# A fifth chunk of weights split early, buffers held per MLP, and a low part moved from POOL to DVE in a three-stage kernel

## The chip, the core and the metric

One core of one Trainium2 chip runs the whole program. The metric is the device time of one execution in microseconds. Engines are named as the profile names them: PE (matrix multiply), DVE (vector), ACT (activation), POOL (GpSimd) and SP (which here only issues DMAs).

## What is computed

Memory attention feeds an MLP with a sigmoid-gated unit, and that feeds a second, normalised and gated MLP. 4 batches of 576 tokens, 8 heads of 64 make 2304 tokens of width 512.

```python
a = softmax(phi, over the sequence)            # 32 memory slots
k_m, v_m = a^T k, a^T v
x = softmax(q k_m^T / 8) v_m                   # (2304, 512)
h = x @ w_in                                   # 512 -> 2048
x = (h * sigmoid(1.702 h)) @ w_out             # 2048 -> 512
xn = x / sqrt(mean(x*x) + 1e-6) * rms_g
g, val = xn @ w_gate, xn @ w_val               # 512 -> 1536
out = (silu(g) * val) @ w_out2                 # 1536 -> 512
```

The inputs are 64-bit floats; the kernel reads them as pairs of 32-bit words and makes 32-bit floats of them on the chip.

## The kernel before, in words

**Numbers.** A 32-bit float operand x is split into a high part (rounded to the format that PE multiplies) and a low part (x minus the high part), and each product is made of three matmuls: high by high, low by high, high by low. So every operand costs one rounding copy, nearly always on ACT, and one subtraction (`sub_lo`, line 125) on DVE or POOL.

**Weights.** `to_f32` makes one 512-column tile of 32-bit weights out of raw words: an absolute value on ACT (line 170), a clamp on POOL (171), and three bit operations on DVE (175, 179, 182). `w_conv` then splits it for the first MLP. For the second MLP a *chunk* is 128 columns of the gate and 128 of the value weights: `b_gate` and `b_val` call `to_f32`, `b_sums` adds four combinations (line 244, four DVE instructions; the second MLP multiplies its 2x2 blocks with seven products in place of eight), and `b_tile` four times splits one tile (`b_split`: a copy on ACT at line 223, a subtraction on POOL) and stores it to DRAM in `cache2`. `b_again` (line 271) loads such a chunk back with four DMAs. There are 12 chunks.

**First MLP.** It runs twice over 8 groups of 256 hidden columns: the first pass for batches 0 and 1, the second for batches 2 and 3. A unit is one group and one quarter of the pass's tokens (288): `a_g1` (line 564, gelu at 570, split at 572 and 125) and, one unit later, `a_g2` (line 593), whose four PSUM tiles DVE adds into `x2` (line 601). `vm_part` makes the attention-weighted first weights of the next group. The first pass has the splitting of the first MLP's weights beside it, the second loads them back.

**Side work.** In the second pass three steps of a generator, `second_side`, are put between `a_g1` and `a_g2` of each unit: the norm of batches 0 and 1 (`norm_sums`, `norm_side`), the seven operands of each batch (`x_side`: four subtractions at line 686, then five splits), and chunks 0 to 3.

**Second MLP.** `b_unit(c, b)` is chunk c for batch b: seven products of six matmuls (line 728), copies on ACT (757, 760, 762), additions on DVE (742, 765, 767), silu on ACT (768), two multiplications on DVE (746, 747), a split of the gated product (749 on ACT, and `sub_lo` into `pl`), and two stores to DRAM. The opening, `units_of(range(NG1), (0, 1), ...)`, runs chunks 0 to 3 for batches 0 and 1, while the list `more` prepares batches 2 and 3: `norm_sums(1)` (squares at 614, column sums on PE at 632), `norm_side` (line 668) and `x_side`. Then chunks 4 to 11 run for all four batches, each beside the splitting of the next chunk; then chunks 0 to 3 for batches 2 and 3; then the last product (line 795).

**Order.** The program is written as one sequence of steps, and the framework lays each engine's queue out ahead of time: of the instructions that are ready in its own simulation it takes the one written first, and `tc.high_priority(n)` counts an instruction as written n instructions earlier. On the chip each queue then runs in that fixed order. Units of the second pass are raised by 150, `vm_next` by 100, units of the opening by 400.

**Buffers.** Tiles come from pools with a fixed number of buffers. `cv` (4 tiles of 576 columns: conversions, norms, sums) and `w` (6 tiles of 1024 columns: split weights) last through the kernel; `vm` (4) belongs to the attention and the first MLP. Pools `raw`, `gf` and `gr` of the first MLP are released at its end, and those of the second (`rawb`, `tmp`, `gpp`, `nxp`, `xbp`) take the same memory, each tile waiting for the tiles that lay there.

Of the kernel before, what the change touches and what calls it, by code (L numbers as in the profile page):

```python
# [18 lines left out]
def kernel(  # L19
# [44 lines left out]
    NA = F1 // FG  # L64
    NB = F2 // FG
    NC2 = F2 // P
    NPRE = 4
    NG1 = 4
    TW = 2 * HALF
    TO = 384  # L70
# [5 lines left out]

    const = ctx.enter_context(tc.tile_pool(name="const", bufs=1))
    bigp = ctx.enter_context(tc.tile_pool(name="big", bufs=6))
    cvp = ctx.enter_context(tc.tile_pool(name="cv", bufs=4))
    dramp = ctx.enter_context(tc.tile_pool(name="dram", bufs=1, space=bass.MemoryType.DRAM))  # L80
    wp = ctx.enter_context(tc.tile_pool(name="w", bufs=6))
    w3p = ctx.enter_context(tc.tile_pool(name="w3", bufs=2))
    smp = ctx.enter_context(tc.tile_pool(name="sm", bufs=4))

# [2 lines left out]
    rawa = tc.alloc_tile_pool(name="rawa", bufs=3, side="right")  # L87
    gfp = tc.alloc_tile_pool(name="gf", bufs=3, side="right")
    grp = tc.alloc_tile_pool(name="gr", bufs=5, side="right")
    vmp = tc.alloc_tile_pool(name="vm", bufs=4, side="right")  # L90
    raws = [rawa]
    ps_mm = ctx.enter_context(tc.tile_pool(name="ps_mm", bufs=3, space=bass.MemoryType.PSUM))
    ps_acc = ctx.enter_context(tc.tile_pool(name="ps_acc", bufs=3, space=bass.MemoryType.PSUM))
    ps_att = ctx.enter_context(tc.tile_pool(name="ps_att", bufs=2, space=bass.MemoryType.PSUM))
# [9 lines left out]
        return bigp.tile([P, 4608], dt, tag="big", name=name)  # L104

    def wtile(name, dt=F32R):
        return wp.tile([P, 1024], dt, tag="w", name=name)

    def ttile(name, dt=F32):
        return cvp.tile([P, TW], dt, tag="cv", name=name)  # L110

    def psum(pool, name):
        tag = {id(ps_mm): "mm", id(ps_acc): "acc", id(ps_att): "att"}[id(pool)]
# [10 lines left out]
    def sub_lo(eng, lo, full, hi):  # L124
        eng.tensor_tensor(out=lo, in0=full, in1=hi.bitcast(F32), op=ALU.subtract)  # L125
# [1 line left out]


    cache = dramp.tile([NA * 4, P, 1024], F32, tag="cache", name="cache")
    cache2 = dramp.tile([NG1 * 4, P, 1024], F32, tag="cache2", name="cache2")  # L130
    pcache = [
        dramp.tile([2, NC2, P, PT], F32, tag=f"pcache{i}", name=f"pcache{i}") for i in range(2)
    ]
# [3 lines left out]
        return [(*key, w, i) for w in ("in", "out") for i in range(2)]  # L137

    def w_load(hf):
        raw = loaded[hf] = raws[0].tile([P, 1024], U32, tag="raw", name="raw_" + "_".join(map(str, hf)))  # L140
        if hf[0] == "b":
            c, w = hf[1:]
            src = {"gate": w_gate, "val": w_val, "o2": w_o2}[w]
            if w == "o2":
                nc.sync.dma_start(out=raw, in_=src[c * P : (c + 1) * P, :])
            else:
                nc.sync.dma_start(
                    out=raw.rearrange("p (k f) -> p k f", k=NE),
                    in_=src[:, 2 * c * P : 2 * (c + 1) * P].rearrange("(k p) f -> p k f", p=P),
                )  # L150
            return
        g, w, i = hf[2:]
        src = {"in": w_in, "out": w_out}[w]
        if w == "out":
            nc.sync.dma_start(out=raw, in_=src[g * FG + i * P : g * FG + (i + 1) * P, :])
        else:
            nc.sync.dma_start(
                out=raw.rearrange("p (k f) -> p k f", k=2),
                in_=src[2 * i * P : 2 * (i + 1) * P, 2 * g * FG : 2 * (g + 1) * FG].rearrange(
                    "(k p) f -> p k f", p=P  # L160
                ),
            )
# [55 lines left out]
    def b_split(c, j, x):  # L218
        n = 256 if j == 3 else 512
        y = b_wtile(c, j)  # L220
        if c >= NPRE:
            wt.setdefault(("b", c), {})[j] = y
        nc.scalar.copy(out=y[:, :n], in_=x)  # L223
        sub_lo(G, y[:, n:], x, y[:, :n])
        if c < NG1:
            nc.sync.dma_start(out=cache2[c * 4 + j][:, : 2 * n], in_=y.bitcast(F32))

    def b_gate(c):
# [21 lines left out]
    def b_steps(c):  # L250
        yield b_gate, c
        yield b_val, c
        yield b_sums, c
        for j in range(4):
            yield b_tile, c, j
# [42 lines left out]

    def ld_phi(u):
        b, g = u  # L300
        if b < 2:
            km = vmp.tile([P, 1024], F32, tag="vm", name=f"kmisc{b}_{g}")
        else:
            km = wtile(f"kmisc{b}_{g}", F32)
        kmisc[u] = km
        dst = km[:CP, 0:768].rearrange("p (t r x) -> p t r x", t=2, r=2)
        for t in range(2):
            nc.sync.dma_start(
                out=dst[:, blk(b, 2 * t) // 2],
                in_=phi[b, 4 * g + 2 * t : 4 * g + 2 * t + 2].rearrange(  # L310
                    "r (p c) m -> p r (c m)", c=C6
                ),
            )
# [204 lines left out]
    def vm_part(pr, g, c):  # L518
        wh, wl = wt["a", pr, g, "in"]
        vh, vl = vL[pr]  # L520
        if c == 0:
            vm[pr, g] = [
                vmp.tile([P, 1024], F32R, tag="vm", name=f"vm{pr}_{g}{x}").rearrange("p (b c f) -> p b c f", b=2, c=2) for x in "hl"
            ]
        hi, lo = vm[pr, g]
        lows = []
        ps = (ps_a("pvm") if start_up[0] else psum(ps_mm, "pvm")).rearrange("p (j f) -> p j f", j=2)
        for j in range(2):
            p_ = 2 * c + j
            w0 = slice(p_ * FG, (p_ + 1) * FG)  # L530
            for i, (a, w) in enumerate(((vh, wh), (vl, wh), (vh, wl))):
                nc.tensor.matmul(  # L532
                    ps[:, j], lhsT=a[:, p_], rhs=w[:, w0], start=(i == 0), stop=(i == 2)
                )


        for rows, bb, src in (
            (slice(0, 64), slice(0, 2), slice(0, 2)),
            (slice(64, 128), 1, 0),
            (slice(64, 128), 0, 1),  # L540
        ):
            o, x = (rows, bb, c), ps[rows, src]
            nc.scalar.copy(out=hi[o], in_=x)
            lows.append((lo[o], x, hi[o]))
        for o, x, h in lows:
            sub_lo(nc.vector, o, x, h)
        if c == 1:
            wt.pop(("a", pr, g, "in"))
# [168 lines left out]
    def b_unit(c, b):  # L717
# [26 lines left out]
        def late_2():  # L744
            prod(px, 6, 6, False, True)
            nc.vector.tensor_tensor(out=pf[:, 1], in0=pf[:, 1], in1=sg[:, 1], op=ALU.mult)
            nc.vector.tensor_tensor(out=pf[:, 0], in0=sg[:, 0], in1=px, op=ALU.mult)  # L747
            ph, pl = (gpp.tile([P, TW], F32R, tag="gp", name=x) for x in ("ph", "pl"))
            nc.scalar.copy(out=ph, in_=fv)  # L749
            sub_lo(G if b < 2 and c < NG1 else V, pl, fv, ph)  # L750
            n = slice((b % 2) * S, (b % 2) * S + S)
            for i, x in enumerate((ph, pl)):
                nc.sync.dma_start(out=pcache[b // 2][i, c, :, n], in_=x.bitcast(F32))
# [95 lines left out]
    def first(n):  # L849
        return tc.high_priority(n) if n else nullcontext()  # L850
# [34 lines left out]
    def second_side():  # L885
        for w in ("gate", "val"):
            yield w_load, ("b", 0, w)
        yield from norm_sums(0)
        yield from b_prep(0, 1)
        yield from norm_side(0)  # L890
        yield from x_side(0, 0)
        yield from b_prep(1, 2)
        yield from x_side(0, 1)
        yield from b_prep(2, 3)
        yield from norm_side(1)
        yield from b_steps(3)
        yield from x_side(1, 0)

    units = [(i, key, t) for i, key in enumerate(groups) for t in range(4)]
    order = [hf for key in groups[1:NA] for hf in halves(key)]  # L900
# [36 lines left out]
    def run(lo, hi, prev, side, per):  # L937
        nonlocal done
        for i, key, t in units[lo:hi]:
            if key == ("a", 1, 0) and t == 1:  # L940
                side, per = second_side(), 3
            if key == ("a", 1, 7) and t == 1:
                b_again(0)
            with first(150 if key[1] else 0):
                a_g1(*key[1:], t)
            if i + 1 < NA:
                w_conv(halves(groups[i + 1])[t])
                done += 1
                if done + ahead <= len(order):
                    w_load(order[done + ahead - 1])  # L950
            elif i + 1 < len(groups) and t in (0, 2):
                w_again((*groups[i + 1], "in" if t == 0 else "out"))
            if t == 2 and i + 1 < len(groups):
                vm_next(*groups[i + 1][1:], 0, 1)
            for s in islice(side, per):
                do(s)
            with first(150 if key[1] else 0):
                a_g2(*prev[1:])
            prev = (*key, t)
        a_g2(*prev[1:])  # L960
        return side

    side = run(8, len(units), ("a", 0, 1, 3), side, 2)
    for pool in (vmp, grp, gfp, rawa, kmp, vlp):
        pool.release()
    two = dict(side="right", reuse_waits="tile")
    raws[0] = rawb = tc.alloc_tile_pool(name="rawb", bufs=2, **two)
    tmp = tc.alloc_tile_pool(name="tmp", bufs=4, **two)
    gpp = tc.alloc_tile_pool(name="gp", bufs=3, **two)
    nxp = tc.alloc_tile_pool(name="nx", bufs=1, **two)  # L970
    xbp = tc.alloc_tile_pool(name="xb", bufs=2, **two)
    for s in (*side, *x_side(1, 1)):
        do(s)

    def units_of(cs, bs, steps, more):
# [55 lines left out]
    for g in range(2 * PT // TO):  # L1031
        p_out(g)
        for x in loads[2 * g + 3 : 2 * g + 5]:
            p_load(*x)
    for pool in (xbp, nxp, gpp, tmp, rawb):
        pool.release()


# [31 lines left out]
```

## Time and profile before

| what | value |
|---|---|
| time, median of 3 runs | 936.31 us (935.64 to 937.98) |
| time of the profiled execution | 942.23 us |
| its span (first to last instruction on the core) | 940.4 us |
| mean granted PE clock, share of full | 0.978 |
| busy share: PE, DVE, ACT, POOL | 91%, 63%, 48%, 52% |
| bytes moved by DMA | 170.14 MB |

The profile is of one execution. Busy is the time in which an engine runs instructions. A wait is an engine's idle time before an instruction, put down to what released it. In the rows below, "x12" counts instructions; "A:B" is a stretch in us from the start of the span; a clock of 1.00 is 2.4 GHz and 0.50 is 1.2 GHz, so a value between is a mix; the last two columns of a stretch are the busy share of the DMA engines and GB/s.

### The profile page before, as it was taken

How to read it: one execution, taken by the hardware profiler on the slowest of the kernel's cores; microseconds unless marked ns; L12 is line 12 of the kernel's file. 1: busy time of each engine (PE TensorE's matmuls, PEld its weight loads, DVE VectorE, ACT ScalarE, POOL GpSimd, SP SyncE). 2: the span in 40 equal slices, each digit the busy share in tenths (PEclk: the TensorE clock that was granted, in tenths of full speed). 3: DMA queues.
4: the chain of work that ended last, by engine and by line, in shares of the span. 5: the costliest groups of instructions: out<-in, count | busy, mean ns of one | idle time of the engine just before them, and what ended most of it. 6: DMA issues, size and time to landing. Idle time of an engine off the chain costs nothing.

```text
span 940.4 us, 16149 instructions
## 1 busy us (share of the span) xinstructions
PE 852.3 (91%) x6008; PEld 803.2 (85%) x6008; DVE 588.4 (63%) x1115; ACT 452.5 (48%) x995; POOL 487.0 (52%) x416
## 2 busy tenths in 40 slices
PE   3877998888999998989998769999999899999997
PEld 2766997887999998889998668999999898888886
DVE  5589777679865369895646989977776774000000
ACT  2257764564657665555455635555565453000000
POOL 2466798789966646863574886533351541000000
PEclk9998999899999999999999979999999999999999
DMA  9984358844532354453626135444446796966661
GB/s 221 229 260 157 114 178 225 261 148 157 171 118 108 109 195 146 168 181 124 223 101 200 64 108 187 150 172 162 148 147 239 255 359 226 344 221 220 211 196 33
DMA packets 86239, 170.14 MB, mean 181 GB/s; under 512 B 6544, under 2 KB 49552, under 8 KB 86160
## 3 DMA queue, kind: packets, MB, share of 16 engines
q1 hardware_dynamic: 81552, 152.33, 50.9%
q10 hardware_dynamic: 4608, 16.78, 4.6%
q8 instruction: 47, 0.77, 0.3%
q14 instruction: 32, 0.26, 0.1%
HBM read 111.94 MB, written 57.15 MB: 180 GB/s over the span
## 4 chain that ended last, share of the span: by engine, by line
PE 55%; DVE 15%; DMA 9%; POOL 7%; issue 5%; ACT 5%; SPq 2%; ACTq 0%; DVEq 0%; POOLq 0%
PE pg L795 16%; PE pg L593 12%; PE px L728 11%; PE pg L564 5%; PE pw L728 5%; POOL cv L171 3%; PE py L728 3%; DVE t L686 2%; DMA stage<-in_q_dram 2%; DVE cv L179 2%; DVE cv L182 2%; DMA raw_a_out<-in_moe_w_out_dram 2%; PE pvm L532 2%; POOL gr L125 2%; DVE x L668 2%
## 5 line engine op out<-in xcount | busy, mean ns | idle before, releaser
L593 PE MATMUL pg<-gr,a_outh 128*128 128x288 f32 x1024 | 239.0, 303 | 12.8 <-DVE x L601 9.7
L593 PEld LDWEIGHTS pg<-gr,a_outh 128*128 128x128 f32 x1024 | 177.3, 192 | 17.2 <-DVE x L601 12.9
L728 PE MATMUL px<-x,b_w 128*128 128x288 f32 x1152 | 175.3, 300 | 16.0 <-DVE pf L747 6.5
L728 PEld LDWEIGHTS px<-x,b_w 128*128 128x128 f32 x1152 | 161.0, 191 | 20.7 <-DVE pf L747 7.6
L125 POOL TENSOR_TENSOR gr<-gf,gr 128x288 fp32r<-128x288 f32 x128 | 117.5, 933 | 80.0 <-ACT gr L572 72.3
L171 POOL TENSOR_SCALAR cv<-cv 128x512 f32<-128x512 f32 x67 | 134.1, 2008 | 38.5 <-ACT cv L170 37.7
L593 PE MATMUL pg<-gr,a_outl 128*128 128x288 f32 x512 | 153.4, 300 | 0.0
L795 PE MATMUL pg<-o,p 128*128 128x512 f32 x648 | 147.6, 389 | 0.0
L795 PEld LDWEIGHTS pg<-o,p 128*128 128x128 f32 x648 | 121.5, 188 | 25.0
L601 DVE TENSOR_TENSOR x<-x,pg 128x288 f32<-128x288 f32 x224 | 97.0, 448 | 63.3 <-PE pg L593 62.1
L728 PE MATMUL pw<-x,b_w 128*128 128x288 f32 x576 | 92.9, 299 | 7.8 <-DVE sg L767 3.7
L593 PEld LDWEIGHTS pg<-gr,a_outl 128*128 128x128 f32 x512 | 98.8, 193 | 0.0
L728 PEld LDWEIGHTS pw<-x,b_w 128*128 128x128 f32 x576 | 82.0, 190 | 9.5 <-DVE sg L767 3.9
L572 ACT CAST gr<-gf 128x288 fp32r<-128x288 f32 x128 | 53.7, 433 | 40.7 <-PE pg L593 35.4
L570 ACT ACTIVATE gf<-pg 128x288 f32<-128x288 f32 x128 | 51.0, 409 | 44.1 <-POOL gr L125 26.6
L804 ACT COPY o<-pg 128x512 f32<-128x512 f32 x18 | 10.6, 588 | 127.2 <-PE pg L795 126.1
L125 POOL TENSOR_TENSOR b_w<-cv,b_w 128x256 fp32r<-128x256 f32 (+1 forms) x24 | 27.9, 1165 | 71.5 <-ACT b_w L223 71.5
L175 DVE TENSOR_SCALAR cv<-cv 128x512 uint32<-128x512 uint32 x68 | 52.0, 765 | 20.2 <-POOL cv L171 20.1
L728 PE MATMUL py<-x,b_w 128*128 128x288 f32 x288 | 47.6, 299 | 0.6 <-DVE sg L765 0.6
L768 ACT ACTIVATE sg<-sg 128x576 f32<-128x576 f32 x48 | 33.0, 687 | 29.3 <-DVE sg L767 29.0
L749 ACT CAST ph<-pf 128x576 fp32r<-128x576 f32 x48 | 32.4, 676 | 28.8 <-DVE pf L747 28.6
L728 PEld LDWEIGHTS py<-x,b_w 128*128 128x128 f32 x288 | 41.8, 192 | 0.9 <-DVE sg L765 0.8
(193 smaller groups left out, 1581.6 us busy)
## 6 DMA issues: line engine op xcount, KB each, us to landing
p<-pcache SPq DMA_DIRECT2D x24, 1152.0 KB, 8.5
pcache<-ph SPq DMA_DIRECT2D x48, 288.0 KB, 2.2
pcache<-pl SPq DMA_DIRECT2D x48, 288.0 KB, 2.7
b_w<-cache SPq DMA_DIRECT2D x24, 512.0 KB, 4.5
raw_a_in<-in_moe_w_in_dram SPq DMA_DIRECT2D x16, 512.0 KB, 4.4
raw_a_out<-in_moe_w_out_dram SPq DMA_DIRECT2D x16, 512.0 KB, 3.3
raw_b_gate<-in_moe_w_gate_dram SPq DMA_DIRECT2D x12, 512.0 KB, 3.9
raw_b_val<-in_moe_w_val_dram SPq DMA_DIRECT2D x12, 512.0 KB, 4.0
```

Of the source, the lines that this page charges most:

```text
L125: eng.tensor_tensor(out=lo, in0=full, in1=hi.bitcast(F32), op=ALU.subtract)
L171: clamp.tensor_scalar(out=t.bitcast(F32), in0=t.bitcast(F32), scalar1=MINW, scalar2=MAXW, op0=ALU.max, op1=ALU.min,)
L175: nc.vector.tensor_scalar(out=t, in0=t, scalar1=3, scalar2=0x3FFFFFFF, op0=ALU.logical_shift_left, op1=ALU.bitwise_and,)
L564: nc.tensor.matmul(ps[:, :HALF], lhsT=a[:, b, c, f], rhs=at[:, y, c, n], start=(i == 0), stop=(i == 5),)
L570: nc.scalar.activation(out=gf[:, :HALF], in_=ps[:, :HALF], func=AF.Gelu_apprx_sigmoid)
L572: nc.scalar.copy(out=gr[:, 0], in_=gf[:, :HALF])
L593: nc.tensor.matmul(ps[:, :HALF], lhsT=wo[a][:, fc, es], rhs=gr[fc][:, y], start=(i == 0), stop=(i == 5),)
L601: nc.vector.tensor_tensor(out=acc[:, e, n], in0=acc[:, e, n], in1=ps[:, :HALF], op=ALU.add)
L728: nc.tensor.matmul(ps, lhsT=w[j][:, o : o + P], rhs=xk[k][:, y, xb], start=(first and i == 0), stop=(i == 5), skip_group_check=not (first ...
L749: nc.scalar.copy(out=ph, in_=fv)
L768: nc.scalar.activation(out=fg, in_=fg, func=AF.Silu)
L795: nc.tensor.matmul(pss[s], lhsT=y[:, a, s * P : (s + 1) * P], rhs=w[:, x * 512 : x * 512 + 512], start=(c == 0 and i == 0), stop=(c == NC2 ...
```

## The change

- `NPRE` goes from 4 to 5: chunk 4 is loaded, split and stored in `second_side` (nine more steps: two loads within `b_prep(3, 4)`, and `b_steps(4)` after `x_side(1, 0)`). In the opening the second unit pair of chunk 3 is now beside `b_again(4)`, four loads, in place of `b_prep(4)`.
- The pools `cv` and `w` exist once for the attention and the first MLP (`cva` with 5, `wa` with 10 tiles, which also hold what lay in `vm`) and once for the second MLP (`cvb` with 4, `wb` with 6). All side steps are done before the first set is released.
- `b_again(0)` is called after the second set is made, no longer in the last group of the second pass.
- The units of the second pass are no longer raised by 150.
- In the opening the low part `pl` is made by DVE, as in the later stages, no longer by POOL.

```diff
-    NPRE = 4
+    NPRE = 5
...
-    cvp = ctx.enter_context(tc.tile_pool(name="cv", bufs=4))
-    wp = ctx.enter_context(tc.tile_pool(name="w", bufs=6))
...
-    vmp = tc.alloc_tile_pool(name="vm", bufs=4, side="right")
+    cva = tc.alloc_tile_pool(name="cva", bufs=5, side="right")
+    wa = tc.alloc_tile_pool(name="wa", bufs=10, side="right")
+    use = dict(raw=rawa, cv=cva, w=wa)
...
-    cache2 = dramp.tile([NG1 * 4, P, 1024], F32, tag="cache2", name="cache2")
+    cache2 = dramp.tile([NPRE * 4, P, 1024], F32, tag="cache2", name="cache2")
...
         sub_lo(G, y[:, n:], x, y[:, :n])
-        if c < NG1:
+        if c < NPRE:
             nc.sync.dma_start(out=cache2[c * 4 + j][:, : 2 * n], in_=y.bitcast(F32))
...
-            sub_lo(G if b < 2 and c < NG1 else V, pl, fv, ph)
+            sub_lo(V, pl, fv, ph)
...
         yield from norm_side(1)
-        yield from b_steps(3)
+        yield from b_prep(3, 4)
         yield from x_side(1, 0)
+        yield from b_steps(4)
...
-            if key == ("a", 1, 7) and t == 1:
-                b_again(0)
-            with first(150 if key[1] else 0):
-                a_g1(*key[1:], t)
+            a_g1(*key[1:], t)
...
-            with first(150 if key[1] else 0):
-                a_g2(*prev[1:])
+            a_g2(*prev[1:])
...
-    side = run(8, len(units), ("a", 0, 1, 3), side, 2)
-    for pool in (vmp, grp, gfp, rawa, kmp, vlp):
+    for s in run(8, len(units), ("a", 0, 1, 3), side, 2):
+        do(s)
+    for pool in (wa, cva, grp, gfp, rawa, kmp, vlp):
         pool.release()
     two = dict(side="right", reuse_waits="tile")
-    raws[0] = rawb = tc.alloc_tile_pool(name="rawb", bufs=2, **two)
+    wb = tc.alloc_tile_pool(name="wb", bufs=6, **two)
+    cvb = tc.alloc_tile_pool(name="cvb", bufs=4, **two)
+    rawb = tc.alloc_tile_pool(name="rawb", bufs=2, **two)
+    use.update(raw=rawb, cv=cvb, w=wb)
...
-    for s in (*side, *x_side(1, 1)):
+    b_again(0)
+    for s in x_side(1, 1):
         do(s)
```

## Rows read from the trace of the kernel before

**Rows 1.** Stretches: length, then busy time of PE, PEld, DVE, ACT, POOL, clock, DMA.

```profile
200.00:240.00 40.00, 34.23 (x279) 32.52 (x278) 33.75 (x62) 24.12 (x54) 34.85 (x32) 0.96 0.43 153
240.00:340.00 100.00, 99.00 (x823) 98.16 (x823) 62.38 (x133) 68.52 (x162) 70.32 (x69) 1.00 0.38 132
340.00:420.00 80.00, 70.50 (x524) 68.33 (x523) 69.32 (x132) 43.88 (x106) 53.33 (x46) 1.00 0.47 169
420.00:486.00 66.00, 65.33 (x500) 65.10 (x500) 39.31 (x81) 32.77 (x76) 36.54 (x38) 1.00 0.39 136
507.00:533.00 26.00, 19.27 (x133) 18.34 (x131) 25.96 (x40) 13.50 (x32) 19.36 (x16) 0.93 0.30 99
533.00:557.00 24.00, 14.29 (x77) 12.54 (x78) 22.59 (x27) 10.00 (x22) 22.39 (x16) 0.79 0.35 118
600.00:740.00 140.00, 139.34 (x1049) 138.59 (x1047) 104.65 (x209) 78.33 (x159) 61.06 (x39) 1.00 0.50 176
```

**Rows 2.** Waits of PE from 486 to 557 us: total, times, longest.

```profile
PE px L728 <- DVE pf L747: 3.8, 1, 3.8
PE px L728 <- DVE pf L742: 2.8, 3, 2.1
PE pw L728 <- ACT b_w L223: 1.7, 1, 1.7
```

**Rows 3.** Groups of DVE, 507 to 557 us: busy us, mean ns, idle before.

```profile
L668 DVE SCALAR_TENSOR_TENSOR x<-x,rg,rb 128x288 f32<-128x288 f32 x12 | 10.2, 885 | 0.4 <-ACT rb L654 0.4
L746 DVE TENSOR_TENSOR pf<-pf,sg 128x288 f32<-128x288 f32 x5 | 6.3, 1270 | 1.2 <-ACT sg L768 1.2
L182 DVE SCALAR_TENSOR_TENSOR cv<-raw_b_gate,cv 128x512 uint32<-128x512 uint32 x1 | 1.5, 1536 | 0.0
L179 DVE SCALAR_TENSOR_TENSOR cv<-raw_b_gate,cv 128x512 uint32<-128x512 uint32 x1 | 1.5, 1530 | 0.0
L175 DVE TENSOR_SCALAR cv<-cv 128x512 uint32<-128x512 uint32 x2 | 1.5, 740 | 0.0
L182 DVE SCALAR_TENSOR_TENSOR cv<-raw_b_val,cv 128x512 uint32<-128x512 uint32 x1 | 1.2, 1165 | 0.0
L179 DVE SCALAR_TENSOR_TENSOR cv<-raw_b_val,cv 128x512 uint32<-128x512 uint32 x1 | 0.9, 926 | 0.0
```

**Rows 4.** Stretch 507 to 557 us, line 244 alone: its DVE busy time.

```profile
507.00:557.00 50.00, 2.62 (x4) 0.86 0.33 108
```

**Rows 5.** Groups of POOL, 507 to 557 us.

```profile
L125 POOL TENSOR_TENSOR pl<-pf,ph 128x576 fp32r<-128x576 f32 x6 | 9.6, 1593 | 4.1 <-ACT ph L749 4.1
L171 POOL TENSOR_SCALAR cv<-cv 128x512 f32<-128x512 f32 x2 | 4.0, 2018 | 0.0
L125 POOL TENSOR_TENSOR b_w<-s,b_w 128x512 fp32r<-128x512 f32 x2 | 2.7, 1385 | 1.0 <-ACT b_w L223 1.0
L125 POOL TENSOR_TENSOR b_w<-cv,b_w 128x512 fp32r<-128x512 f32 (+1 forms) x2 | 2.3, 1192 | 0.0
```

**Rows 6.** Tile pl, whole span: ns min/median/max; then who waited for it.

```profile
L125 DVE TENSOR_TENSOR pl<-pf,ph x40: 745/753/1223, 569.8 to 798.6; 128x576 fp32r<-128x576 f32 x40
L125 POOL TENSOR_TENSOR pl<-pf,ph x8: 1417/1523/1843, 494.6 to 553.2; 128x576 fp32r<-128x576 f32 x8
  ACT pf L760: 19.2, 23
```

**Rows 7.** Lines 668 and 746, whole span: ns min/median/max.

```profile
L668 DVE SCALAR_TENSOR_TENSOR x<-x,rg,rb x28: 504/512/1683, 349.0 to 530.9; 128x288 f32<-128x288 f32 x28
L746 DVE TENSOR_TENSOR pf<-pf,sg x48: 444/459/1684, 492.7 to 791.6; 128x288 f32<-128x288 f32 x48
```

**Rows 8.** Timeline of ACT, POOL and PE: start, length.

```profile
472.07 0.69 ACT L614 ACTIVATE sq<-x 128x576 f32<-128x576 f32 x1 [0.45 <-DVE x L601]
490.72 0.81 POOL L125 TENSOR_TENSOR sr<-sq,sr 128x288 fp32r<-128x288 f32 x1 [0.54 <-ACT sr L622]
501.08 0.42 PE L632 MATMUL pnm<-ones_r,sr 128*96 128x2 f32 x4
```

More of the change, by code (lines that the diff above doesn't have):

```diff
@@ L89 @@
     grp = tc.alloc_tile_pool(name="gr", bufs=5, side="right")
-    vmp = tc.alloc_tile_pool(name="vm", bufs=4, side="right")
-    raws = [rawa]
+    cva = tc.alloc_tile_pool(name="cva", bufs=5, side="right")
+    wa = tc.alloc_tile_pool(name="wa", bufs=10, side="right")
+    use = dict(raw=rawa, cv=cva, w=wa)
     ps_mm = ctx.enter_context(tc.tile_pool(name="ps_mm", bufs=3, space=bass.MemoryType.PSUM))
@@ L106, in wtile @@
     def wtile(name, dt=F32R):
-        return wp.tile([P, 1024], dt, tag="w", name=name)
+        return use["w"].tile([P, 1024], dt, tag="w", name=name)
     def ttile(name, dt=F32):
-        return cvp.tile([P, TW], dt, tag="cv", name=name)
+        return use["cv"].tile([P, TW], dt, tag="cv", name=name)
     def psum(pool, name):
@@ L139, in w_load @@
     def w_load(hf):
-        raw = loaded[hf] = raws[0].tile([P, 1024], U32, tag="raw", name="raw_" + "_".join(map(str, hf)))
+        raw = loaded[hf] = use["raw"].tile([P, 1024], U32, tag="raw", name="raw_" + "_".join(map(str, hf)))
         if hf[0] == "b":
@@ L300, in ld_phi @@
         b, g = u
[L301 to L305, printed above, removed]
+        km = kmisc[u] = wtile(f"kmisc{b}_{g}", F32)
         dst = km[:CP, 0:768].rearrange("p (t r x) -> p t r x", t=2, r=2)
@@ L522, in vm_part @@
             vm[pr, g] = [
-                vmp.tile([P, 1024], F32R, tag="vm", name=f"vm{pr}_{g}{x}").rearrange("p (b c f) -> p b c f", b=2, c=2) for x in "hl"
+                wtile(f"vm{pr}_{g}{x}").rearrange("p (b c f) -> p b c f", b=2, c=2) for x in "hl"
             ]
@@ L1034 @@
             p_load(*x)
-    for pool in (xbp, nxp, gpp, tmp, rawb):
+    for pool in (xbp, nxp, gpp, tmp, rawb, cvb, wb):
         pool.release()
```

## The prediction

> **What bounds the kernel now.** I first cut the span into stretches and looked for those in which PE does not run through [rows 1]. From 600 to 740 us it does: 139.34 of 140 us busy, 1049 matmuls, 7.49 a microsecond, and this with DVE at 104.65 of 140. The first MLP's second pass runs up to 486 us. In its first half (340 to 420) PE is idle for 9.5 of 80 us while DVE is busy for 69.32; in its second half (420 to 486) PE lacks 0.7 of 66 us and DVE has 26.7 us free. The opening of the second MLP is the worst place: from 507 to 557 us PE ran 210 matmuls where 50 us at 7.49 hold 375. The missing 165 are 22 us, made of 16.4 us of idle time and of a clock at 0.93 and then 0.79 of full. DVE is busy for 25.96 of 26 and 22.59 of 24 us there, POOL for 19.36 and 22.39.
>
> The waits of PE before those gaps name DVE lines, above all the last product that waits for line 747 and the one behind line 742, and once the split of chunk 4's weights on ACT [rows 2]. In that stretch DVE's own waits are 1.2 and 0.4 us in the groups shown [rows 3]: its queue is full, and PE's additions and multiplications stand in it behind the preparation of batches 2 and 3 and of chunk 4. So the opening is bound by DVE, and the change is to be priced there as DVE time.
>
> DVE is also slow there. Lines 668 and 746 have medians of 512 and 459 ns over the whole span but maxima near 1.68 us [rows 7], and means of 885 and 1270 ns in this stretch [rows 3], where POOL is busy for 41.8 of 50 us [rows 1]. The twelve and five instructions took 16.5 us where medians would make 12 x 0.512 + 5 x 0.459 = 8.4: 8.1 us of stretching.
>
> **Chunk 4 leaves the opening.** Its bit operations and sums took 1.5 + 1.5 + 1.5 + 1.2 + 0.9 = 6.6 us in lines 175, 179 and 182 [rows 3] and 2.6 us in line 244 [rows 4]: DVE loses 9.2 us of work. POOL loses two clamps and four low parts, 4.0 + 2.7 + 2.3 = 9.0 us [rows 5]. PE's 1.7 us wait for the chunk's split goes too [rows 2]; I count it within the DVE sum, since the split was late because DVE was. In their place stand four loads of `b_again(4)` on SP, which the opening already does for chunks 1 to 3; their price I bound by 0 and that same 1.7 us, and take 0. Chunk 5's conversion comes next, with one more whole chunk of units to cover it.
>
> **The low part moves from POOL to DVE.** Six of the eight lie in the stretch. POOL loses 9.6 us [rows 5]; DVE gains 6 x 0.753 = 4.5 us by the median of the forty that it makes later [rows 6]. The bound above: if each were stretched as line 746 was, by 1270/459 = 2.77 [rows 3, 7], they would cost 6 x 2.09 = 12.5 us. I take 4.5, by the later rows of the same instruction. The wait changes its owner: `pl` now waits in DVE's queue for ACT's rounding, with the next unit's additions queued behind it, and ACT's copy into `pf` waits for it to free its buffer (19.2 us in 23 waits over the later stages, where PE still runs through) [rows 1, 6].
>
> **Less stretching.** POOL loses 9.6 + 9.0 = 18.6 of its 41.8 us, 45%. The relief on the 8.1 us lies between 0 and all of it; I take the share, 3.6 us.
>
> The opening's sum: -9.2 + 4.5 - 3.6 = -8.3 us. At best -9.2 + 4.5 - 8.1 = -12.8; at worst -9.2 + 12.5 = +3.3. As DVE hardly idles there, I let PE gain what DVE does; the ceiling is the 22 us.
>
> **Chunk 4 enters the second pass, and the raise goes.** The side work grows from 82 steps to 91; three a unit over 31 units give 93 places, so all still fits ahead of the pass's end. At most 9.2 us of DVE and 9.0 us of POOL come into 420 to 486 us, where DVE has 26.7 and POOL 29.5 us free [rows 1]: that is the cover, and without it all 9.2 us would land on PE through line 601, which empties PE's accumulators. Four stores and two loads move along on SP. Taking away the raise lets side steps stand ahead of line 601 and of gelu. The first pass runs without a raise: from 240 to 340 us PE lost 1.0 of 100 us with DVE 62% busy, from 200 to 240 us 5.8 of 40 (14%) with DVE 84% busy. The raised pass lost 12% at 87% [rows 1]. So at like DVE load raised and unraised passes lose alike, and load is what counts. With chunk 4 the second half has (39.3 + 9.2)/66 = 73%, half way between; idle time grows late in that range, so I take a third of the way, 5% of 66, less the 0.7 us lost now: +2.5 us. Bounds: 0, and +7.1 if 420 to 486 lost as 340 to 420 does (66 x 9.5/80 - 0.7).
>
> **The handover.** The second set of `cv` and `w` lies on memory of the first MLP's tiles. `b_again(0)` is issued later in the text, but lies on buffers of the attention and of raw words, free before the last group ends; the first units' `tmp` tiles wait for the last `cv` tiles; the squares of `norm_sums(1)`, which begin at 472.07 us, may have to wait for `gf` and `gr` tiles, so until about 486. That is 14 us. The last of these sums ended at 491.5 and PE took it up at 501.08 [rows 8], so 9.5 us are slack, and 4.5 could show if all moved by 14. I take +1, bounds 0 and 14 (no slack). Merging `vm` into ten `w` tiles and giving `cv` a fifth can reorder the first pass too; I bound that by the 5.8 us idle in 200 to 240 in either direction [rows 1] and take 0.
>
> **Sum.** -8.3 + 2.5 + 1 = -4.8 us. The profiled execution took 942.23 us (span 940.4 and 1.8 around it), so it would take 937.4. It lies 5.9 us above the median of the runs; the same difference on 936.31 gives 931.5 us.
>
> **Rivals.**
>
> *The opening fills up.* If the last preparation of batch 3 comes forward by the whole of chunk 4's work, PE could get back all 22 us: -22 + 3.5 = -18.5, 918. For it: DVE is the only named cause of the large gaps. Against it: the norm and `x_side` of batches 2 and 3 remain, stretched, and they hold DVE at 99.8% already before chunk 4 comes (507 to 533) [rows 1].
>
> *DVE gets back what it gave.* Moving work from POOL to DVE only changes who holds the other up. If half of the six low parts are stretched and nothing else is relieved, they cost 3 x 2.09 + 3 x 0.753 = 8.5 us against 9.2: -0.7, and with the costs of the pass and the handover up to +2.8: 935.6 to 939.1, no change. For it: line 746 takes up to 1.684 us, about as long as one low part on POOL (1.593) [rows 5, 7], as if DVE waited out a whole POOL instruction. Against it: 45% of POOL's work goes, and the forty low parts on DVE never took more than 1.223 us [rows 6]. The Trainium skill has this as a rule: in "SBUF — State Buffer", section "Who interferes with whom", a DVE instruction with two SBUF inputs and a GpSimd instruction that reads SBUF contend, and whoever comes first holds the pair of ports for its whole instruction. "Perfetto Trace Analysis", section "Optimizing Scalar/DVE Operations", draws the consequence that moving work between the two engines might not help; by that, the move alone is worth nothing, and the sum would be this rival's. The stretched rows agree with the lock; no row shows yet what the move is worth.
>
> *The second pass pays (the other side).* Without the raise, side steps on DVE stand ahead of line 601. If 340 to 420 us lost its 9.5 us twice and 420 to 486 lost at the same rate (+7.1), that is +16.6: -8.3 + 1 + 16.6 = +9.3, 945.6. It decides, that is ends slower by over 0.3%, once the pass loses more than 8.3 - 1 + 2.8 = 10.1 us more than now. For it: DVE is 87% busy in the first half. Against it: the equal losses of raised and unraised stretches, and 26.7 free microseconds [rows 1].
>
> *The handover is late.* With 4.5 to 14 us more before batch 2 is ready: -8.3 + 2.5 + 4.5 = -1.3 (935.0) up to +8.2 (944.5). For it: every pool of the second set lies on tiles in use until the end. Against it: the 9.5 us of slack.
>
> **How the numbers follow.** What a measurement of this kernel can tell from no change is 0.3%, 2.8 us: 933.5 to 939.1. Chances: the forecast (923.5 to 933.5) 0.41; the opening fills up 0.12; DVE gets it back 0.20; a late handover 0.10, half of it unchanged and half slower; the second pass pays 0.14; the first pass slower by its new buffers 0.03. Faster 0.41 + 0.12 = 0.53, same 0.20 + 0.05 = 0.25, slower 0.05 + 0.14 + 0.03 = 0.22. The range goes to 918, the second case's price, and to 944, short of the last two cases' full prices; I leave about 0.07 outside at each end. The likeliest case alone has 923.5 to 933.5.
>
> **What would show it.** Right: between about 500 and 560 us PE runs clearly more than 210 matmuls in 50 us, the clock stays near 1.00, lines 175, 179 and 182 are absent until chunk 5, and lines 668 and 746 have means well under 885 and 1270 ns. In 420 to 486 us chunk 4's conversions appear and PE stays within 3 us of full. The port rival shows as low parts on DVE near 2 us; the pass's as waits of line 593 for line 601 above today's; the handover's as squares that begin after 486 us and PE idle between the last line 593 and the first runs of line 728. I am wrong if the gaps of the opening stay with chunk 4 gone, or if a stage that I left at zero, the first pass or everything behind 600 us, moves by more than 3 us.

## The result, and the profile after

The changed kernel takes 922.86 us (median of 4 runs, 920.66 to 930.07), the kernel before 936.92 beside it (4 runs, 935.64 to 937.98): a ratio of 0.9855 [0.9814, 0.9896], 14.1 us less. The profiled execution took 930.07 us (span 928.3), the longest of its four runs, against 942.23 of the one before: 12.2 us less. Lines of the later functions have moved up by five: 593 is now 588, 601 is 596, 668 is 663, 728 is 723, 742 is 737, 746 is 741, 747 is 742; of the earlier ones 564 is 559, 614 is 609, and the helpers have moved by one (125 is 124, 171 is 170, 175 is 174, 182 is 181, 223 is 222).

The same stretches as in [rows 1], and the one from 486 to 507 us, of the changed kernel; columns as there.

```profile
200.00:240.00 40.00, 32.78 (x258) 31.40 (x257) 33.14 (x55) 20.11 (x44) 34.31 (x29) 0.91 0.40 138
240.00:340.00 100.00, 99.33 (x827) 98.66 (x826) 62.73 (x130) 73.09 (x168) 60.10 (x64) 1.00 0.35 125
340.00:420.00 80.00, 71.92 (x519) 69.87 (x519) 74.05 (x135) 42.96 (x102) 51.64 (x47) 0.98 0.53 182
420.00:486.00 66.00, 64.94 (x485) 64.02 (x484) 40.29 (x80) 29.42 (x73) 34.08 (x35) 1.00 0.44 163
486.00:507.00 21.00, 21.00 (x164) 20.72 (x163) 13.57 (x24) 14.48 (x30) 14.67 (x13) 1.00 0.62 210
507.00:533.00 26.00, 21.59 (x159) 20.19 (x158) 23.82 (x41) 17.02 (x35) 14.52 (x12) 1.00 0.51 178
533.00:557.00 24.00, 19.82 (x140) 18.41 (x138) 19.58 (x39) 12.57 (x26) 15.95 (x11) 1.00 0.26 96
600.00:740.00 140.00, 138.74 (x1048) 138.26 (x1046) 103.39 (x207) 77.96 (x160) 59.67 (x37) 1.00 0.54 189
```

From 507 to 557 us PE ran 299 matmuls, against 210. It was idle for 8.6 us in place of 16.4, at the full clock (2.4 GHz) in place of 0.93 and 0.79. DVE was busy for 43.4 us (48.6 before), POOL for 30.5 (41.8).

DVE's groups in the same stretch of the changed kernel, to be held against [rows 3]: total us, mean ns of one, idle before.

```profile
L663 DVE SCALAR_TENSOR_TENSOR x<-x,rg,rb 128x288 f32<-128x288 f32 x12 | 8.3, 728 | 0.7 <-ACT rb L649 0.7
L124 DVE TENSOR_TENSOR pl<-pf,ph 128x576 fp32r<-128x576 f32 x6 | 5.3, 881 | 3.4 <-ACT ph L744 2.5 <-DMA pcache<-ph 0.8
L741 DVE TENSOR_TENSOR pf<-pf,sg 128x288 f32<-128x288 f32 x7 | 4.0, 569 | 0.1
L174 DVE TENSOR_SCALAR cv<-cv 128x512 uint32<-128x512 uint32 x2 | 2.1, 1026 | 1.1 <-POOL cv L170 1.1
```

Lines 663 and 741 take 728 and 569 ns where they took 885 and 1270, six low parts on DVE cost 5.3 us, and DVE now has idle time. Line 174 belongs to chunk 5.

PE's waits from 486 to 557 us in the changed kernel (as [rows 2]): total, times, longest.

```profile
PE px L723 <- DVE pf L742: 3.6, 3, 2.1
PE px L723 <- ACT sg L752: 1.7, 1, 1.7
PE px L723 <- DVE pf L737: 1.2, 2, 0.9
```

The wait for chunk 4's split is gone; what remains still names mostly DVE.

To place the 12.2 us I counted matmuls in both traces and took the ends of the same work. The first pass ends at 304.8 us in both. The second pass takes 180.7 us (181.5), and from there to the end of chunk 5, sixteen units of 42 matmuls, 106.3 (115.2). Chunks 6 to 11 take 134.4 (134.1), chunks 0 to 3 for batches 2 and 3 take 58.2 (61.2), the last product 138.3 in both. So 8.9 us came from the opening and chunk 5. The 3.0 us of the last part belong to this one execution of the kernel before, whose clock fell to half (1.2 GHz) for 3.4 us at 742.4: in the other traces with the old pools the same part takes 57.6 to 58.7.

That stretch, end of second pass to end of chunk 5, is the measure for the experiments. It repeats well: the changed kernel and three of the variants below (r3, x2, x4) take 106.2 to 106.6. Before:

```profile
486.20:601.40 115.20, 95.83 (x669) 91.27 (x668) 96.77 (x155) 62.62 (x131) 75.37 (x55) 0.94 0.45 150
```

Changed:

```profile
485.60:591.90 106.30, 95.21 (x692) 90.54 (x692) 90.32 (x159) 65.78 (x135) 64.02 (x49) 1.00 0.48 165
```

PE's idle time fell from 19.4 to 11.1 us, DVE's work by 6.5, POOL's by 11.4.

### The profile page after: what moved, and what is told of

Same layout as the page of the kernel before. It is cut to its first block, busy times and chain, and to the rows that moved or that the text cites. A ratio compares the mean times of both kernels' runs of the same rounds, so it can differ in the third digit from the quotient of the medians.

```text
span 928.3 us, 16192 instructions
## 1 busy us (share of the span) xinstructions
PE 842.1 (91%) x6008; PEld 793.0 (85%) x6008; DVE 594.9 (64%) x1123; ACT 455.3 (49%) x997; POOL 475.2 (51%) x408
## 4 chain that ended last, share of the span: by engine, by line
PE 55%; DVE 18%; DMA 11%; ACT 5%; issue 5%; POOL 4%; SPq 2%; ACTq 0%; DVEq 0%; POOLq 0%
PE pg L790 16%; PE pg L588 12%; PE px L723 10%; PE pg L559 6%; PE pw L723 5%; DMA raw_a_out<-in_moe_w_out_dram 4%; PE py L723 3%; DVE cv L178 2%; POOL cv L170 2%; DMA pcache<-ph 2%; DVE cv L174 2%; DVE x L596 2%; DVE cv L181 1%; DVE x L663 1%; DMA kmisc<-in_phi_dram 1%
## 5 line engine op out<-in xcount | busy, mean ns | idle before, releaser
L588 PE MATMUL pg<-gr,a_outh 128*128 128x288 f32 x1024 | 235.5, 304 | 20.0 <-DVE x L596 17.0
L588 PEld LDWEIGHTS pg<-gr,a_outh 128*128 128x128 f32 x1024 | 174.3, 191 | 25.6 <-DVE x L596 20.9
L723 PE MATMUL px<-x,b_w 128*128 128x288 f32 x1152 | 172.9, 297 | 12.5 <-DVE pf L742 6.1
L723 PEld LDWEIGHTS px<-x,b_w 128*128 128x128 f32 x1152 | 157.9, 188 | 17.5 <-DVE pf L742 8.0
L124 POOL TENSOR_TENSOR gr<-gf,gr 128x288 fp32r<-128x288 f32 x128 | 112.5, 891 | 69.4 <-ACT gr L567 67.9
L723 PE MATMUL pw<-x,b_w 128*128 128x288 f32 x576 | 90.5, 296 | 0.8 <-DVE sg L762 0.8
L124 DVE TENSOR_TENSOR pl<-pf,ph 128x576 fp32r<-128x576 f32 x48 | 39.8, 829 | 15.6 <-ACT ph L744 8.1
```

Of the source, the lines that this page charges most:

```text
L588: nc.tensor.matmul(ps[:, :HALF], lhsT=wo[a][:, fc, es], rhs=gr[fc][:, y], start=(i == 0), stop=(i == 5),)
L723: nc.tensor.matmul(ps, lhsT=w[j][:, o : o + P], rhs=xk[k][:, y, xb], start=(first and i == 0), stop=(i == 5), skip_group_check=not (first ...
```

## The experiments

The prediction made a sum of the parts, each with a price of its own. The rival theory is that they work only together, through buffers and the queues' order. The first four kernels do one part alone, the next four take one part out of the changed kernel, the last four try what the traces of these pointed to. The parts of the change are here chunk 4's early split, the low parts on DVE, the missing raise, and "the pools", by which I mean the two sets of buffers together with the later place of `b_again(0)`. Each ratio is to the kernel before on the same chip, with its 95% interval; traces are of one execution each.

### One part alone

**Chunk 4 alone** (kernel before, its pools, raise and POOL's low parts kept).

```diff
-    NPRE = 4
+    NPRE = 5
...
-        yield from b_steps(3)
+        yield from b_prep(3, 4)
         yield from x_side(1, 0)
+        yield from b_steps(4)
```

> The kernel before with the fifth chunk split in the second pass and nothing else changed. Theory A (the opening is bound by DVE, and chunk 4's conversion is most of what it sheds): the opening loses 9.2 us of DVE work and 9.0 us of POOL work, so 6 to 11 us faster than before, about 928. Theory C (the gain is that of the buffers, which let work start earlier everywhere): within 3 us of before, 934 to 940, since the four old cv buffers hold the extra chunk back and the second pass pays what the opening gains.

Measured: 937.68 us, ratio 0.9983 [0.9961, 1.0005]: nothing. Its stretch from the end of the second pass to the end of chunk 5:

```profile
480.20:595.60 115.40, 101.00 (x685) 95.85 (x684) 82.26 (x141) 60.85 (x125) 67.96 (x52) 0.93 0.48 159
```

DVE has 14.5 us less work there than before, and the stretch is as long as before. Two things in the trace go with this; neither was tried apart. First, ACT's waits from 440 to 500 us in this kernel:

```profile
ACT b_w L223 <- DMA cache<-b_w: 5.9, 2, 3.0
```

Two copies of the splits, the last of chunk 3 and the last of chunk 4, wait for one of the six `w` tiles until a store of it to DRAM has landed. Chunk 4's four copies are laid about a unit apart, at 458.5, 464.2, 470.7 and 476.8 us, where the changed kernel has them done by 461.6 and none waits. Between them SP loads weights with `b_again` (line 271, at 453.1, 458.0 and twice from 462.1) into the same six tiles, since `b_again(0)` still stands in the last group here. That the queue was spread out because the tiles are short is my reading; the waits are shown. Second, the preparation of batches 2 and 3 is late: line 668 begins 41.1 us after the second pass (20.8 before). The same stretch cut in four:

```profile
480.20:505.00 24.80, 24.80 (x195) 24.80 (x194) 9.96 (x21) 14.03 (x28) 12.91 (x12) 1.00 0.82 268
505.00:535.00 30.00, 27.60 (x210) 26.78 (x208) 20.38 (x36) 16.95 (x34) 14.59 (x12) 1.00 0.49 164
535.00:565.00 30.00, 20.88 (x116) 18.30 (x115) 25.96 (x44) 15.61 (x33) 21.60 (x17) 0.89 0.22 80
565.00:595.60 30.60, 27.72 (x171) 25.97 (x170) 25.96 (x42) 14.27 (x30) 18.86 (x13) 0.83 0.47 143
```

DVE has room up to 535 us and PE runs almost through. Then the preparation meets chunk 5's conversion, DVE fills to 87%, PE drops to 116 matmuls in 30 us, and the clock falls. The hole was moved, not closed. How much each of the two brings is open.

**Low parts on DVE alone.**

```diff
-            sub_lo(G if b < 2 and c < NG1 else V, pl, fv, ph)
+            sub_lo(V, pl, fv, ph)
```

> The kernel before with the low part of the gated product on DVE in the opening and nothing else changed. Theory A: DVE gains 4.5 us of work and is relieved of stretching by 9.6 of POOL's 41.8 us (1.9 us), so 2 to 4 us slower, about 939.5. Theory B (the port rival: whoever holds the port holds the other up, and moving work between the two changes nothing): within 2 us of before. A gain of over 3 us would contradict both and say that the chain through POOL was the slow one.

Measured: 937.08, 0.9981 [0.9961, 1.0000]. The stretch from the second pass to the end of chunk 5 is 2.0 us shorter, with DVE busier by 1.9 and POOL less by 11.2:

```profile
485.60:598.80 113.20, 97.69 (x668) 93.52 (x667) 98.65 (x163) 62.82 (x131) 64.13 (x47) 0.92 0.46 153
```

The eight low parts took 10.0 us on DVE, not the 6.0 that the prediction's 0.753 us makes: three of them lasted 1.82 to 1.96 us, the sign that the prediction named for its port rival. As DVE's work grew by only 1.9 net, it won back some 8.1 us elsewhere. And although DVE had more work, PE gained 2.0.

**Pools alone** (changed kernel with chunk 4, raise and low parts as before).

```diff
-    NPRE = 5
+    NPRE = 4
...
-            sub_lo(V, pl, fv, ph)
+            sub_lo(G if b < 2 and c < NG1 else V, pl, fv, ph)
...
+            with first(150 if key[1] else 0):
```

> The changed kernel with four chunks, the low part on POOL in the opening and the raise of the second pass: of the change only the pools per MLP, the later loading of chunk 0 and the merged ten w tiles remain. Theory A: 0 to 2 us slower than before, 937 to 939. Theory C: the first unit of the first MLP starts 8 us earlier in the changed kernel's trace, so 5 to 10 us faster than before, about 930.

Measured: 938.24, 0.9995 [0.9961, 1.0029]. Two opposite effects: this execution's second pass ends at 475.0 us (486.2 before), and the stretch behind it takes 121.3 us (115.2), where PE waits twice for chunk 4's split, which DVE and ACT have not yet made:

```profile
PE px L723 <- ACT b_w L222: 6.5, 1, 6.5
PE pw L723 <- ACT b_w L222: 4.5, 1, 4.5
```

**Raise away alone.**

```diff
-            with first(150 if key[1] else 0):
-                a_g1(*key[1:], t)
+            a_g1(*key[1:], t)
...
-            with first(150 if key[1] else 0):
-                a_g2(*prev[1:])
+            a_g2(*prev[1:])
```

> The kernel before without the raise of the second pass's units and nothing else changed. The prediction's step (load counts, not the raise): within 3 us of before, 934 to 940. Its rival (side steps stand ahead of line 601): 5 to 15 us slower, 942 to 952.

Measured: 943.64, 1.0060 [1.0036, 1.0083], 5.3 us more. The second pass alone takes 5.4 us more, 186.9 against 181.5; the other parts of this execution differ by -2.7 to +1.6. PE's first wait there, 302 to 489 us:

```profile
PE pg L593 <- DVE x L601: 9.2, 9, 2.6
```

The same before, from 304.8 to 486.2 us:

```profile
PE pg L593 <- DVE x L601: 5.4, 4, 1.9
```

The four ratios together, 0.9983, 0.9981, 0.9995 and 1.0060, make +0.2%; all parts at once make -1.45%. That the parts add up is refuted.

### One part taken out of the changed kernel

```diff
r1  NPRE = 4, chunk 4 back in the opening
r2  sub_lo(G if b < 2 and c < NG1 else V, pl, fv, ph)
r3  with first(150 if key[1] else 0):  around a_g1 and a_g2
r4  the kernel before, with all of the change but the pools; b_again(0) stays in the last group
```

> The changed kernel with chunk 4 back in the opening (four chunks split in the second pass), all else as changed. Theory A: 6 to 11 us slower than the changed kernel, 929 to 934. Theory C: within 3 us of the changed kernel, about 923 to 926.

Measured: 937.07, 1.0004 [0.9979, 1.0030]. Without chunk 4's early split the whole gain is gone. The stretch to the end of chunk 5 takes 117.7 us, and PE's longest wait in it, 5.2 us, is for chunk 4's split (line 222):

```profile
PE px L723 <- ACT b_w L222: 5.2, 1, 5.2
474.20:591.90 117.70, 101.47 (x692) 96.11 (x691) 100.16 (x170) 68.37 (x141) 73.81 (x55) 0.93 0.42 142
```

> The changed kernel with the low part of the gated product back on POOL in the opening. Theory A: DVE loses 4.5 us of work in the opening and is stretched a little more, so 2 us faster to 1 us slower than the changed kernel, 921 to 924. Theory B: the same as the changed kernel. Slower by over 3 us would say that the path through POOL was a bound of its own.

Measured: 932.28, 0.9944 [0.9924, 0.9963]: the low parts on DVE are worth 0.9% (8.3 us) here, against 0.2% alone. Of that 2.4 us lie up to the end of chunk 5 (108.6). The rest is in chunks 6 to 11, where this edit changes no instruction:

```profile
591.70:732.30 140.60, 136.12 (x1010) 133.70 (x1009) 105.00 (x200) 76.19 (x159) 55.32 (x38) 1.00 0.47 162
```

The same work in the changed kernel:

```profile
591.90:726.30 134.40, 133.77 (x1010) 133.30 (x1009) 99.41 (x200) 75.02 (x156) 58.15 (x37) 1.00 0.49 174
```

As many DVE instructions take 5.6 us longer. What differs is the order: in r2's trace the same instructions of these chunks stand in another order on PE, DVE, ACT and POOL. r1 has yet another order and 139.0 us; r3 and x4, with the changed kernel's order on PE, DVE and POOL, take 134.4 and 134.5. One order does not always give one time: r4 and the kernel with chunk 4 alone share theirs and take 138.8 and 136.2. So some 6 of the 8.3 us go with queues that the edit made the framework lay differently, far behind it, and are no price of the low parts in the opening.

> The changed kernel with the second pass's units raised by 150 again. The prediction's step (load counts): within 3 us of the changed kernel. If the raise pushes side work into the opening: 4 to 8 us slower, 927 to 931. If the missing raise cost PE time in the second pass: 3 to 8 us faster, 915 to 920.

Measured: 926.01, 0.9881 [0.9855, 0.9907]. It cannot be told from the changed kernel: the intervals overlap, and with the raise put back the kernel is between about 2 us faster and 7 us slower (0.26% with both intervals' widths). In this one execution the second pass takes 177.8 us, against 180.7 without the raise.

> The kernel before with the fifth chunk, the low part on DVE and no raise, but with the old pools (four cv and six w tiles for the whole kernel, four vm tiles): all of the change but its buffers. Theory A: within 3 us of the changed kernel, 920 to 926, or a little faster since the handover costs nothing. Theory C: 5 to 10 us slower than the changed kernel, 928 to 933.

Measured: 941.40, 1.0054 [1.0036, 1.0072]. The pools, worth nothing alone, are worth 2.0% (18.6 us) to the other parts. The copies of line 223 wait again for stores to DRAM (5.0 us in 2 waits) and the stretch to chunk 5's end is 110.5 us, 4.2 more. The traces place only part of the rest: 4.4 us in chunks 6 to 11 (138.8), 1.1 in the second pass (181.8). The profiled executions lie 8.4 us apart, the changed kernel's being its slowest and this one its fastest.

### What the handover costs, and which buffers matter

In the changed kernel the squares of batches 2 and 3 begin 5.2 us ahead of the second pass's end (14.2 before), the last low part of the sums is ready 20.8 us behind it (5.3), and line 663 begins 27.0 us behind it (20.8). If that delay sets the opening, an earlier preparation should shorten it.

```diff
x1, x3: what lies on the memory freed first
-    wb = tc.alloc_tile_pool(name="wb", bufs=6, **two)
     cvb = tc.alloc_tile_pool(name="cvb", bufs=4, **two)
+    wb = tc.alloc_tile_pool(name="wb", bufs=6, **two)
x2, x3: norm_2, norm_3 of batches 2 and 3
+        with first(800 * pr):
+            step(pr, t)
x4:
-    cva = tc.alloc_tile_pool(name="cva", bufs=5, side="right")
+    cva = tc.alloc_tile_pool(name="cva", bufs=4, side="right")
```

> The changed kernel with the two second pools made in the other order, so that the four new cv tiles lie where the attention's tiles lay (free before the last group) and no longer on gf and gr. In the changed kernel the squares of batches 2 and 3 begin 5.2 us ahead of the second pass's last matmul and the last column sum is ready 20.8 us behind it; before the change it was 14.2 ahead and 5.3 behind. Theory D (the preparation of batches 2 and 3 sets the end of the opening, and the handover delays it): squares again about 14 us ahead, 3 to 6 us faster than the changed kernel, 917 to 920. If the opening is bound by DVE's work alone: within 2 us of the changed kernel.

Measured: 930.97, 0.9936 [0.9906, 0.9967], slower than the changed kernel. The sums are ready earlier, 10.3 us after the second pass, but now chunk 0's weights load late: six of the first eight loads of line 270 go out only at the pass's end (from 481.7 us; in the changed kernel all eight are out by 451), and the first unit ends 11.0 us after the pass (3.2). Line 663 begins at 28.8 us, no sooner than in the changed kernel.

> The changed kernel with norm_2 and norm_3 of batches 2 and 3 raised by 800, ahead of the opening's units, which are raised by 400. In the changed kernel PE takes up the last sum 2.8 us after it is ready, in the kernel before 9.8 us, in the fifth chunk alone 19.7 us. Theory D: the gap closes, so 1 to 3 us faster than the changed kernel. If DVE alone binds: no change.

Measured: 924.56, 0.9875 [0.9836, 0.9914], no difference from the changed kernel. But line 663 begins 27.0 us after the pass, as there, so this run did not bring the preparation forward and says nothing on the theory.

> The changed kernel with both: new cv tiles on free memory and the sums and the norm's transposes raised. Line 668 for batch 2 then starts about 10 us behind the second pass's end, in place of 27. Theory D: 5 to 12 us faster than the changed kernel, 911 to 918. If DVE's work alone binds the opening: 0 to 2 us faster, since the same work only begins earlier and stands in the way of the units sooner.

Measured: 931.73, 0.9930 [0.9904, 0.9956]. The last column sum is on PE 13.9 us and line 663 begins 18.2 us after the second pass, 9 us sooner than in the changed kernel. It is the only run that brings the preparation forward, and its first unit is late too (it ends at 12.1 us). From the end of the first unit to the end of chunk 5 it takes 102.2 us against 103.1, though line 663 begins 6.1 us after that first unit in place of 23.8. This one execution speaks against the norm's delay holding the opening; a run without the late weights was not made.

> The changed kernel with four cv tiles in the first set in place of five, the ten w tiles kept. Chunk 4's conversion holds four cv tiles from its clamp to its split. If the fifth cv tile is what the old pools lacked: most of their loss comes back, 6 to 15 us slower than the changed kernel. If the ten shared w tiles are: within 3 us of the changed kernel.

Measured: 921.11, 0.9822 [0.9792, 0.9853]. Faster than the kernel before, and the interval overlaps the changed kernel's. The stretch to chunk 5's end is the same:

```profile
477.80:584.10 106.30, 96.51 (x693) 92.11 (x692) 90.13 (x159) 65.65 (x135) 63.97 (x49) 0.98 0.50 165
```

So the fifth `cva` tile is worth nothing that shows. What is left of the pools' effect are the ten joint `w` tiles, a second set made only behind the first MLP, and `b_again(0)` behind it, which in the old place loads chunk 0 into the tiles that chunk 4's split waits for; these three were not tried apart.

## Why the prediction was right, and where its sizes were off

The forecast was 931.5 us, faster by 4.8; measured were 14.1. So the direction and the place of the gain came true, the size did not: 922.86 lies just below the 923.5 to 933.5 that the prediction gave its likeliest case, above the 918 of "the opening fills up". The opening paid 8.9 us and not 22, so that rival is not what happened.

- **What bounds the opening: right for the whole change, the close number partly luck.** Predicted -8.3 us, measured -8.9 (115.2 to 106.3). The longest wait of [rows 2] fell from 3.8 to 2.1 us, the wait for the split is gone, the clock stayed at 1.00, and the 299 matmuls are well over 210. That "PE gains what DVE does" is no rule, though: with chunk 4 alone DVE lost 14.5 us of work and PE gained none, with the low parts alone DVE's work grew by 1.9 us and PE still gained 2.0. And 4.2 of the 8.9 us come only with the pools (r4), to which the sum gave no gain there.
- **Chunk 4 leaves, and less stretching: right.** DVE's work up to chunk 5's end fell by 6.5 us net. Eight low parts came in at 0.968 us on average, 7.7 us, so 14.2 us went out; -9.2 and -3.6 make 12.8. Lines 663 and 741 alone, by their means, gave back 12 x 0.157 + 7 x 0.701 = 6.8 us of stretching.
- **Low parts on DVE: their cost right, their effect on PE not.** The six from 507 to 557 us cost 5.3 us, predicted 4.5 with 12.5 as the bound. But the sum's terms price the move as a loss (4.5 us of work less 1.9 of the 3.6 of relief, POOL's 9.6 us being about half of its 18.6), while PE gained 2.0 us in that stretch with the move alone and loses 2.4 without it (r2). The port rival's sign does not appear in the whole change, where no low part of the opening took over 1.231 us; with the move alone it does (three of 1.82 to 1.96 us), and there the time hardly moved, as that rival says (0.9981). DVE's longest line 663 is 1.302 us now, 1.683 before [rows 7]. The Trainium skill's "Perfetto Trace Analysis", section "Optimizing Scalar/DVE Operations", says that moving work between these two engines might not help; the move alone agrees (0.9981), within the change r2's stretch shows 2.4 us for it, and there the measurement decides.
- **Second pass, +2.5: the mechanism right, the size off.** It measured -0.7. The waits for line 601 did grow as the rival said: 8.3 us in 10 waits from 340 to 486 us. In the old pools, with the raise alone gone, the pass took 5.4 us more, so that raised and unraised stretches lose alike, read from two different passes in [rows 1], does not hold there. The pools gave it back: the pass takes 176.4 us with them alone, and 180.7 with chunk 4 and no raise, +4.3 where +2.5 was predicted (one execution each). PE's waits from 340 to 486 us in the changed kernel:

```profile
PE pg L588 <- DVE x L596: 8.3, 10, 3.3
PE pg L559 <- DVE vm_3l L124: 0.8, 2, 0.6
```

Before, 2.5 us of wait for `vm_5l` stood beside the 5.4 for line 601 in this pass.

- **Handover, +1: no cost seen.** The squares came 9 us and line 663 6 us later, PE ran through from 486 to 507 us (21.00 of 21), and x3, one execution, shows no cost of the delay.
- **The pools in the first pass, 0: the likeliest term that was mis-sized.** The first unit's first matmul of line 559 (564) ends 60 to 63 us after the start in all nine kernels with the new pools, at 64 to 70 in the five with the old. The first pass ends at 299.6 us in the mean of the nine (294.5 to 304.8) and at 303.1 of the five (300.1 to 304.8). That is -3.5 us, one execution each and overlapping; if it holds, it is over the 3 us that the prediction named as a sign of being wrong. With it the sum would be -8.9 - 0.7 - 3.5 = -13.1, near the 14.1 measured. In the profiled execution of the changed kernel this gain does not show (304.8 in both): it lost some 8 us from 184 to 212 us, as the last section shows.
- **The form of the sum failed.** The prediction added prices that exist only together: chunk 4's early split pays nothing without the pools (0.9983 alone, r4 1.0054), and the pools pay only where that split is out of the opening (0.9995 alone, r1 1.0004). That the opening's total came near rests on the change being made whole.

## What to carry to other kernels

Work taken off the engine that binds a stage pays only if everything that must take its place is there in time: look which buffers the moved work waits for in its new place, and where the work behind it lands then. A part measured alone at nothing may still be needed; take each part out of the whole as well as putting it in alone, and look whether the queues behind the edit still have the same order, before a difference there is put down to it. A buffer rule and an order of work that are changed together are to be priced together.

## What the runs showed of the hardware

One execution can lose some 8 us more in a stretch than another that runs the same queues. The changed kernel and x2 have the same order on PE and DVE up to the opening, yet their first passes end at 304.8 and 295.4 us. The changed kernel's clock was at half (1.2 GHz) from 38.4 to 55.5 us and x2's was not (1.00 over 38 to 68 us), but that is not the cause: at 60 us the changed kernel is 1.1 us ahead. Some 8 us of the difference arise in one stretch of the same matmuls, in the changed kernel:

```profile
183.70:211.90 28.20, 21.47 (x131) 20.67 (x130) 25.89 (x41) 16.36 (x31) 21.86 (x20) 0.82 0.39 139
```

and in x2:

```profile
182.40:202.60 20.20, 17.28 (x129) 16.58 (x129) 18.42 (x38) 15.97 (x31) 18.48 (x16) 1.00 0.56 184
```

Here two bit operations on DVE, with both inputs in SBUF (the on-chip memory of the tiles), took 2.96 and 4.95 us (start, length):

```profile
196.14 2.96 DVE L181 SCALAR_TENSOR_TENSOR cv<-raw_a_in,cv 128x512 uint32<-128x512 uint32 x1
200.56 4.95 DVE L178 SCALAR_TENSOR_TENSOR cv<-raw_a_in,cv 128x512 uint32<-128x512 uint32 x1
```

In x2 the same two took 0.67 and 1.21:

```profile
192.98 0.67 DVE L181 SCALAR_TENSOR_TENSOR cv<-raw_a_in,cv 128x512 uint32<-128x512 uint32 x1
196.20 1.21 DVE L178 SCALAR_TENSOR_TENSOR cv<-raw_a_in,cv 128x512 uint32<-128x512 uint32 x1
```

POOL ran beside them without a gap:

```profile
198.51 2.48 POOL L170 TENSOR_SCALAR cv<-cv 128x512 f32<-128x512 f32 x1
200.97 2.50 POOL L124 TENSOR_TENSOR a_outl<-cv,a_outh 128x512 fp32r<-128x512 f32 x2
203.43 1.53 POOL L124 TENSOR_TENSOR gr<-gf,gr 128x288 fp32r<-128x288 f32 x2
```

POOL's last instruction ended at 205.0 us, the long one on DVE at 205.5. So a DVE instruction lasted here through four POOL instructions in a row, none of them over 1.3 us; the prediction had it wait out one. PE waited 5.3 us for line 596 behind them, and its clock was 0.82. That POOL held DVE up is read from the times (POOL's are rough); no run tried it. All seven two-input instructions of DVE over 2.3 us in the 14 traces lie beside POOL instructions that follow one another in this way, in five of the traces at other places (2.4 to 3.4 us).

The four runs of the changed kernel spread over 9.4 us, and the kernel before does so too (932.83 to 946.32 in 35 runs on another chip), so a single profile of either is a poor measure of stages outside the opening.
